# Sparse attention and gated MLP on one core: selection rows issued from ScalarE's queue, pair 0's clamp and subtraction moved, one transposed block on TensorE, a new order

## The chip, the cores and the metric

The kernel runs on 1 core of one Trainium2 chip. The metric is the device time of one execution in microseconds (us), lower is better. Its engines, as the profile names them: PE (TensorE matmuls; PEld its weight loads), DVE (VectorE), ACT (ScalarE), POOL (GpSimd) and SP (SyncE, which here only issues DMAs). An engine name with a q (SPq, ACTq) is a DMA issue on that engine's instruction stream.

## The reference, cut to what matters

```python
# attention: q, k, v are [4, 8, 768, 64]; chunks of 32 keys, nc = 24, top_k = 6
k_min, k_max = min / max of k over each chunk
ub = sum_d max(q * k_min, q * k_max)            # upper bound of a chunk for a query
ub = where(causal over chunks, ub, -1e9)
top_chunks = the 6 best chunks of each query
scores = where(chunk chosen and causal, q @ k.T / 8, -1e9)
x = softmax(scores) @ v                         # heads side by side: [4, 768, 512]
# gated MLP of x
h = gelu_tanh(x @ w_in); u, v = halves of h     # w_in [512, 1024]
v_n = (v - mean) / sqrt(var + 1e-6) * g_ln
v_s = w_sg @ v_n + b_sg                         # over the 768 positions of a batch
out = x + (u * v_s) @ w_out
```

## The kernel before, in words

The 32 heads are worked on as 16 pairs (p = 0 to 15, four pairs to a batch b). For each pair the K side (`kside`) transposes k by TensorE (`ktr`) or by a VectorE block transpose (`kbt`), takes chunk minima and maxima into the tile W (`kmm` or `kmmr`, VectorE), copies k to bf16 (`kev`, `kevh`), and subtracts the minima from the maxima (`wsub`, line 639, on POOL). The Q side (`qside`) transposes q (`qtr`), copies it from PSUM to qT (`qev`), clamps it at zero from below into rT (`rel`, line 662, on POOL, reading qT), and casts it (`qcast`). The bound is then two matmuls, qT by the minima plus rT by the differences (`ub`). VectorE transposes it (`utr`), finds the eight best of each query (`m8`), compares (`dn`) and transposes the result back into the tile Dt (`dt`, line 774).

From pair 4 on pairs go two at a time through the selection (`select_full`), and a DMA brings each head's rows of Dt into the score operand QA: `qd`, line 779, four for each couple of pairs, 24 in all, 36 KB each. The score matmuls (`sc`, line 820, three tiles of 1024, 1024 and 640 columns for each head of the pair) wait for them, ScalarE takes the exponential (`exp`, line 826), POOL zeroes above the diagonal (`aff`), TensorE multiplies by v (`pv`, `pvd`, lines 898 and 905), and VectorE divides into XS (`rcp`, line 913, and `xs`, line 915). For each pair `xtrans` transposes the 128 columns of x into xT: by six TensorE transposes and a VectorE copy (`xtr`, `xev`), or, for the blocks listed in XDMA, by one DMA transpose on SP's queue (line 924).

After every fourth pair the MLP of that batch follows: `hv` (line 947) and `gv` (gelu) for the gate half, `bns`, `bna`, `var`, `rstd` and `vhat` for the normalisation, `hu` (line 998) and `gu` for the other half, `pt` (line 1015, w_sg by vhat, which needs all six vhat of its batch), `vs` and `gt` or `gtp` for the gating, `ou` (line 1060) and `os` (line 1072) for the output, `st` for its store. Stores of batches 0 to 2 are issued on ScalarE's queue, those of batch 3 on SP's.

Nothing of this order is left to the program text. The functions only record operations, each with an engine, the tiles that it reads and writes, and a name (its tag). The five lists in TABLE give the order on each engine, as numbers of operations in the order of recording; `slots` gives the PSUM buffer of each tile (four buffers of 512 columns for most, two of 1024 for the scores). `link` puts in the semaphore waits that the order makes necessary. Every engine's list, SP's and ScalarE's DMA issues among them, is worked in order: what waits holds all that stands behind it.

Of the kernel before, what the change touches and what calls it, by code (L numbers as in the profile page):

```python
# [260 lines left out]
def _build(nc, ctx, q, k, v, w_in, g_ln, w_sg, b_sg, w_out, out):  # L261
# [55 lines left out]
    XDMA = tuple((2, d) for d in range(NDK)) + tuple((3, d) for d in range(3))  # L317
# [412 lines left out]
    def select_full(pairs, u, v_):  # L730
# [21 lines left out]
        for hf, t in enumerate(ts):  # L752
            for d0, d1 in ((0, 128),) if hf == 0 else ((0, 64), (64, 128)):
                s0 = (d0 + 64 * hf) % 128
# [3 lines left out]
                    dve(NH, 190), ("utr", pairs[0], hf), reads=[t], writes=[("U", u, hf, d0)], ps=[t])  # L758
# [23 lines left out]

    def mask_rows(w):

        for i in range(2):
# [7 lines left out]
            else:  # L793
# [3 lines left out]
                 gps(S // 2, 150), ("mrow", w, i, 2), shift=(i == 0), writes=[("QD", w, i)] + ([("QA", w, 0, 0), ("QA", w, 0, 1)] if i == 0 else []))  # L797

    def scores_full(p):
# [6 lines left out]
        for i in range(2):  # L806
            for c, c0 in enumerate(range(0, ETOT, 1024)):
# [10 lines left out]
                def sc(e, t=t, mms=mms, i=i):  # L818
                    for (o, n, kb, q0) in mms:
# [456 lines left out]
```

## Time and profile before

| | us |
|---|---|
| median of 3 runs | 214.81 |
| the runs | 214.98, 212.99, 214.81 |
| the profiled execution: its own time | 211.83 |
| the profiled execution: first to last instruction (span) | 209.7 |
| PE busy | 193.1 (92%) |
| DVE busy | 185.0 (88%) |
| ACT busy | 155.5 (74%) |
| POOL busy | 126.9 (61%) |

The profile is one execution; 2.1 us of its own time lie outside its span. Busy time of PE is the time in which at least one matmul was under way; matmuls are pipelined, so a row of the trace can be longer than what one more such instruction would add. The chain of waits follows the work that ended last back from the end, so the length of a piece in it is net of overlap. All times below count from the start of the span. The granted TensorE clock was 1.000 of full speed throughout.

### The profile page before, as it was taken

The page shows a single profiled execution, that of the slowest core. Times are in us where ns is not written, and L with a number is a line of the kernel's source. Part 1 is how long each engine was busy: PE and PEld are TensorE (multiplying, and loading weights), DVE is VectorE, ACT ScalarE, POOL GpSimd, SP SyncE. Part 2 cuts the span into 40 slices and gives each one's busy share as a digit, 9 for nine tenths or more (in the row PEclk, how much of TensorE's full clock was granted, in tenths as well). Part 3 has the DMA queues.
Part 4 walks back from the last instruction along what each step waited for, and adds up shares of the span by engine and source line. Part 5 has one row for each costly group of instructions (what it writes and reads, how often), then busy time and mean ns, then how long its engine had stood idle before and what let it go on. Part 6 is the DMA issues. An engine that isn't in the chain of part 4 may idle for free.

```text
span 209.7 us, 5781 instructions
## 1 busy us (share of the span) xinstructions
PE 193.1 (92%) x2254; PEld 125.7 (60%) x2254; DVE 185.0 (88%) x507; ACT 155.5 (74%) x221; POOL 126.9 (61%) x179
## 2 busy tenths in 40 slices
PE   7789979889999998999997999987998999899993
PEld 2446757664675775985554766763655667455652
DVE  4698999999999999999999999999798347598994
ACT  3479969974899986998898768987999974563000
POOL 7376869678378989796633597988603695111000
PEclk9999999999999999999999999999999999999999
DMA  7999999959899989979999679894006054011226
GB/s 150 219 218 237 238 289 283 322 115 201 188 197 164 216 133 185 178 138 225 205 192 167 164 153 232 138 197 104 2 7 137 0 91 137 29 74 50 100 101 252
DMA packets 106891, 33.71 MB, mean 161 GB/s; under 512 B 100976, under 2 KB 102000, under 8 KB 106864
## 3 DMA queue, kind: packets, MB, share of 16 engines
q1 hardware_dynamic: 104272, 28.62, 69.3%
q10 hardware_dynamic: 2592, 4.72, 7.0%
q8 instruction: 18, 0.29, 0.6%
q14 instruction: 9, 0.07, 0.1%
HBM read 24.77 MB, written 6.29 MB: 148 GB/s over the span
## 4 chain that ended last, share of the span: by engine, by line
PE 39%; DVE 36%; DMA 11%; ACT 5%; issue 4%; SPq 3%; DVEq 0%; POOL 0%
PE PSG L1015 8%; PE PSG L947 6%; PE PSG L1060 5%; PE PSG L998 5%; PE PSC L820 5%; DMA QA<-Dt 5%; DVE m L766 4%; DVE U L755 3%; DVE W L619 3%; DVE vgb L1036 3%; DVE XS L915 3%; DMA bsgbc<-in_moe_b_sg_dram 3%; DVE KA L791 3%; PE PSG L572 3%; PE PSG L898 2%
## 5 line engine op out<-in xcount | busy, mean ns | idle before, releaser
L826 ACT ACTIVATE E<-PSC 128x1024 bf16<-128x1024 f32 (+1 forms) x72 | 62.8, 915 | 9.7 <-PE PSC L820 8.7
L820 PE MATMUL PSC<-QA,KA 128*128 128x128 bf16 (+2 forms) x336 | 37.7, 246 | 1.8 <-DMA QA<-Dt 1.4
L1015 PE MATMUL PSG<-wsgT,vhat 128*128 128x384 bf16 x192 | 34.5, 326 | 1.4 <-DVE vhat L987 1.4
L820 PEld LDWEIGHTS PSC<-QA,KA 128*128 128x128 bf16 x336 | 23.6, 98 | 12.3 <-ACT E L826 4.5
L1040 POOL TENSOR_TENSOR uT<-vgb,uT 128x384 bf16<-128x384 f32 x24 | 22.4, 947 | 9.5 <-DVE vgb L1036 9.3
L669 POOL CAST QA<-qT 64x768 bf16<-64x768 f32 (+1 forms) x28 | 23.4, 838 | 4.0 <-DVE qT L646 2.1
L1015 PEld LDWEIGHTS PSG<-wsgT,vhat 128*128 128x128 bf16 x192 | 18.0, 98 | 12.5 <-DVE vhat L987 1.9
L998 PE MATMUL PSG<-xT,winb 128*128 128x384 bf16 x128 | 23.7, 326 | 1.2 <-DMA xT<-XS 1.2
L1003 ACT ACTIVATE uT<-PSG 128x384 bf16<-128x384 f32 x32 | 14.5, 489 | 12.9 <-PE PSG L998 12.5
L831 POOL TENSOR_SCALAR_AFFINE_SELECT E<-E 128x768 bf16<-128x768 bf16 x24 | 20.6, 863 | 5.8 <-ACT E L826 5.5
L875 ACT ACTIVATE E<-PSC 128x1024 bf16<-128x1024 f32 (+1 forms) x24 | 21.2, 917 | 3.5 <-PE PSC L866 3.5
L1060 PE MATMUL PSG<-woutb,uT 128*128 128x512 bf16 (+1 forms) x100 | 23.7, 370 | 0.0
L947 PE MATMUL PSG<-winb,xT 128*128 128x512 bf16 x96 | 22.2, 379 | 1.4 <-DVE xT L464 0.8
L965 POOL TENSOR_TENSOR rstd<-rstd,neghalf 128x3 f32<-128x3 f32 x8 | 7.3, 916 | 24.9 <-DVE rstd L963 24.8
L951 ACT ACTIVATE vgb<-PSG 128x512 f32<-128x512 f32 x24 | 13.8, 598 | 9.3 <-PE PSG L947 9.2
L898 PE MATMUL PSG<-vx,E 128*128 128x65 bf16 x480 | 19.8, 194 | 0.2
L619 DVE TENSOR_REDUCE W<-PSG 128x12 f32<-128x384 f32 x32 | 16.1, 544 | 3.8 <-POOL W L395 2.7
L898 PEld LDWEIGHTS PSG<-vx,E 128*128 128x128 bf16 x480 | 17.2, 98 | 3.0 <-DVE vgb L1036 0.5
L1036 DVE SCALAR_TENSOR_TENSOR vgb<-PSG,glnT,bsgbc 128x384 f32<-128x384 f32 x24 | 14.3, 605 | 5.3 <-PE PSG L1015 5.2
L998 PEld LDWEIGHTS PSG<-xT,winb 128*128 128x128 bf16 x128 | 12.0, 98 | 10.5 <-DMA xT<-XS 1.4
L956 DVE BATCH_NORM_STATS2 stats<-vgb 128x6 f32<-128x512 f32 x24 | 15.7, 678 | 2.2 <-ACT vgb L951 2.1
L915 DVE TENSOR_TENSOR XS<-PSG,rden 128x384 bf16<-128x384 f32 x32 | 17.2, 550 | 0.4
(94 smaller groups left out, 374.8 us busy)
## 6 DMA issues: line engine op xcount, KB each, us to landing
vn<-in_v_dram SPq DMA_DIRECT2D x16, 384.0 KB, 5.1
qn<-in_q_dram SPq DMA_DIRECT2D x24, 192.0 KB, 4.5
out_dram<-osb ACTq DMA_DIRECT2D x18, 256.0 KB, 2.5
kn<-in_k_dram SPq DMA_DIRECT2D x16, 192.0 KB, 4.5
kn<-in_k_dram SPq DMA_DIRECT2D x32, 96.0 KB, 4.0
uT<-in_moe_w_sg_dram SPq DMA_DIRECT2D x4, 384.0 KB, 5.2
vgb<-in_moe_w_in_dram SPq DMA_DIRECT2D x3, 512.0 KB, 5.6
qn<-in_q_dram SPq DMA_DIRECT2D x16, 96.0 KB, 3.9
```

What stands on the lines that cost most here:

```text
L619: P.op("dve", lambda d, m=m, op=op, src=src, h0=h0, h1=h1: d.tensor_reduce(W[w][:, m, 12 * h0:12 * h1].rearrange("p (h c) -> p h c", h=h1 ...
L669: P.op("pool", lambda g, i=i, r0=r0, r1=r1: g.tensor_copy(QA[w][i or 0][r0:r1, :], qT[r][r0:r1, :]), gps(S, 250 if i == 1 else 150), ("qca ...
L820: r = e.matmul(t.ap()[:, o:o + n], KA[w][i][:, 128 * kb:128 * kb + 128], QA[w][i][:, q0:q0 + n], start=True, stop=True)
L826: P.op("act", lambda e, t=t, c0=c0, c1=c1, i=i: e.activation(E[es][:, i, c0:c1], t.ap()[:, 0:c1 - c0], ACTF.Exp, scale=SCALE), act(c1 - c0 ...
L875: P.op("act", lambda e, t=t, c0=c0, c1=c1, n=n: e.activation(E[es][:, :, c0:c1], t.ap().rearrange("p (i x) -> p i x", i=2)[:, :, 0:n], ACT ...
L898: r = e.matmul(t.ap()[:, 65 * qb:65 * qb + 65], E[es][:, i, a:a + 128], vx[w][:, kb, i, :], start=first, stop=False, skip_group_check=True)
L915: P.op("dve", lambda d: d.tensor_tensor(XS[:, b % 2, hh // 2, :, i * DH:(i + 1) * DH], pv3()[:, :, 0:DH], rden[rs][:].rearrange("p (j o) - ...
L947: r = e.matmul(t.ap()[:, 0:F], xT[s][:, dk, 128 * qt:128 * qt + 128], winb[:, dk, F:DFF], start=(dk == 0), stop=(dk == NDK - 1))
L998: r = e.matmul(t.ap()[:, 0:TG], winb[:, dk, 128 * fb:128 * fb + 128], xT[s][:, dk, TG * tg:TG * tg + TG], start=(dk == 0), stop=(dk == NDK ...
L1015: r = e.matmul(t.ap()[:, 0:TG], vhat[s][:, sb, 128 * fb:128 * fb + 128], wsgT[:, sb, TG * tg:TG * tg + TG], start=(sb == 0), stop=(sb == N ...
L1040: P.op("pool", lambda g, xg=xg, tg=tg, fb=fb: g.tensor_tensor(gT[s][:, fb, TG * tg:TG * tg + TG], xg, uT[s][:, fb, TG * tg:TG * tg + TG], ...
L1060: r = e.matmul(t.ap()[:, 0:c1 - c0], gT[s][:, fb, 128 * qt:128 * qt + 128], woutb[:, fb, c0:c1], start=(fb == 0), stop=(fb == NF - 1))
```

## The change

- QDQ, the pairs whose `qd` rows ScalarE's queue issues, was empty and now holds pairs 4 to 15: all 24 go from SP's list to ScalarE's.
- RELA = (0,): pair 0's clamp is two Relu activations on ScalarE that read q's transposes in PSUM (`rela0,0` of 192 columns, `rela0,1` of 384), where it was one POOL instruction that read qT.
- WSD = (0,): pair 0's subtraction is on VectorE, where it was on POOL.
- XDMA loses (3, 2): block 2 of batch 3 (pair 14) is transposed by TensorE and copied by VectorE. It had seven blocks and has six.
- The bookkeeping name of a head's rows is split in two (QD with 0 and 1); with ROT = 0 both are written by the same DMA, as before. LQ, LK and ROT are new switches that are off.
- All five lists, and the PSUM buffers, are new.

```diff
-    XDMA = tuple((2, d) for d in range(NDK)) + tuple((3, d) for d in range(3))
+    XDMA = ((2, 0), (2, 1), (2, 2), (2, 3), (3, 0), (3, 1))
...
-    QDQ = ()
-    RELA = ()
-    WSD = ()
+    QDQ = (4, 5, 6, 7, 8, 9, 10, 11, 12, 13, 14, 15)
+    LQ = ()
+    LK = ()
+    RELA = (0,)
+    ROT = 0
+    WSD = (0,)
...
                 P.op("act" if p in QDQ else "sp", lambda e, w=w, i=i, g0=g0: e.dma_start(
                     QA[w][i][g0:g0 + 32, LO:S], Dt[v_][g0:g0 + 32].rearrange("p a b -> p (a b)")), dmac(590),
-                    ("qd", p, i), reads=[("Dt", v_)], writes=[("QD", w, i)], dma=f"qd{w}_{i}", xfer=150)
+                    ("qd", p, i), reads=[("Dt", v_)], writes=[("QD", w, i, 0), ("QD", w, i, 1)], dma=f"qd{w}_{i}", xfer=150)
...
```

The lists themselves, read back into tags. A name is followed by pair or batch, then head and piece. First ScalarE up to pair 0's exponentials; the init names are constant set-up (init10 and 11 copy the tile IND, which POOL finishes with `init8` and `init9`; init21 copies 32 columns):

```
before  init22 init21 init12 qev0,0 qev0,1 kev0,0 kev1,1 init11 kev1,0 qev1,1 qev1,0 init10 kev0,1 exp0,0
after   init22 init10 qev0,0 init21 rela0,0 rela0,1 qev0,1 kev0,0 init12 init11 kev0,1 kev1,1 kev1,0 qev1,0 qev1,1 exp0,0
```

On PE both lists begin ktr0,0 ktr0,1 qtr0,0 qtr0,1 ktr1,1 ktr1,0 ub0, and ub0 has the PSUM buffer that ktr0,0 had. ktr1,0 now has the buffer of qtr0,1. On POOL two memsets of 64x384 that stood behind `init9` now stand ahead of it. VectorE's list has kmm1,1,1 kmm1,0,0 kmm1,0,1 kmm1,1,0 utr0,0.

Where the `qd` rows stand on ScalarE's list, by the number of exponentials ahead of the first row of each couple of pairs:

```
pairs           4,5   6,7   8,9   10,11   12,13   14,15
exps ahead       24    33    45      57      69      83
```

VectorE around `dt14`, `rcp12` and batch 2's normalisation:

```
before  ... bns2,0 rcp12,1 bns2,1 xs12,1 utr14,0 utr14,1 bna2,1 ufix14 rcp12,0 utr14,1 xs12,0 m814,0 m814,1 kevh15,1 dn14 bna2,0 dt14 ...
after   ... bns2,0 bns2,1 bna2,0 bns2,2 utr14,0 utr14,1 utr14,1 ufix14 m814,1 m814,0 dn14 bna2,1 dt14 bna2,2 var2,0 bns2,4 bns2,3 kevh15,1 bna2,3 vhat2,2 rcp12,1 vhat2,0 vhat2,1 xs12,1 ...
```

PE from the first `pt2` to the first `hv3`:

```
before  pt2,0,0 pt2,1,0 sc14,1,0 sc14,0,0 pv13,0 pvd13,0 pt2,1,2 pt2,1,1 sc15,0,0 pt2,0,1 sc14,1,2 pt2,0,2 sc14,0,1 sc14,0,2 pt2,0,3
        sc15,0,1 pv14,1 pvd14,1 pv14,0 pvd14,0 sc15,1,2 sc15,0,2 pt2,1,3 pv15,1 pvd15,1 pv15,0 pvd15,0 ou2,1 ou2,0 xtr3,3 ou2,2 hv3,0
after   pt2,0,3 pt2,0,0 pt2,1,0 pt2,0,1 sc15,1,2 sc14,0,0 pt2,1,3 sc15,1,0 pvd14,1 pt2,1,1 sc14,0,2 pt2,0,2 sc15,0,1 sc15,0,0 pv14,0
        pvd14,0 pv15,1 pvd15,1 sc15,0,2 pt2,1,2 pv15,0 pvd15,0 xtr3,2 ou2,1 xtr3,3 ou2,2 hv3,0
```

## Rows read from the trace of the kernel before

**Rows 1.** Busy time by stretch: us, PE, PEld, DVE, ACT, POOL, clock, DMA, GB/s

```profile
13.00:50.00 37.00, 32.70 (x605) 23.38 (x606) 35.03 (x113) 29.65 (x42) 29.30 (x39) 1.00 1.04 243
50.00:100.00 50.00, 48.84 (x572) 34.03 (x571) 49.40 (x129) 44.09 (x67) 39.28 (x54) 1.00 0.98 181
100.00:143.00 43.00, 40.80 (x483) 26.48 (x482) 42.32 (x115) 36.44 (x48) 29.22 (x38) 1.00 0.97 183
143.00:163.00 20.00, 18.03 (x194) 10.98 (x193) 17.46 (x56) 18.68 (x26) 8.53 (x12) 1.00 0.20 45
163.00:177.00 14.00, 13.83 (x192) 10.23 (x190) 7.42 (x17) 11.08 (x14) 10.18 (x12) 1.00 0.30 72
```

**Rows 2.** Timeline (start, us, engine, line), vhat of batch 2 and first pt2

```profile
160.10 1.91 DVE L987 TENSOR_SCALAR vhat<-vgb,mv,rstd 128x512 bf16<-128x512 f32 x4
...
162.06 2.12 PE L1015 MATMUL PSG<-wsgT,vhat 128*128 128x384 bf16 x12
```

**Rows 3.** DMA queue's own waits on SP: us in total, times, longest

```profile
SPq L779 <- DVE Dt L774: 14.5, 2, 14.2
```

**Rows 4.** The lines 779 and 1078: duration ns min/median/max; issue to landing of line 779

```profile
L779 SPq DMA_DIRECT2D QA<-Dt x24: 507/590/1666, 53.6 to 158.7; - x24
...
DMA to landing us min/median/max: 1.8/2.5/3.9
...
L1078 ACTq DMA_DIRECT2D out_dram<-osb x18: 338/338/452, 93.5 to 201.3; - x18
```

**Rows 5.** Timeline, a store issued by ScalarE between two exponentials

```profile
174.38 0.70 ACT L826 ACTIVATE E<-PSC 128x640 bf16<-128x640 f32 x1 [0.43 <-PE PSC L820]
...
174.66 0.34 ACTq L1078 DMA_DIRECT2D out_dram<-osb  x1
...
174.99 0.70 ACT L826 ACTIVATE E<-PSC 128x640 bf16<-128x640 f32 x1
```

**Rows 6.** Timeline, ScalarE and VectorE where Dt of pairs 6 and 7 is ready

```profile
72.44 1.59 ACT L826 ACTIVATE E<-PSC 128x640 bf16<-128x640 f32 x2
...
73.26 0.78 DVE L774 STREAM_TRANSPOSE Dt<-Dn 128x576 bf16<-128x576 bf16 x1
```

**Rows 7.** Timeline of the start

```profile
3.95 0.21 ACT L440 ACTIVATE CMw<-CMw 64x32 bf16<-64x32 bf16 x1
...
4.55 0.41 POOL L796 MEMSET QA<- 64x384 uint32 x1
...
5.77 0.84 ACT L425 ACTIVATE IND<-IND 32x768 bf16<-32x768 bf16 x1 [1.61 <-POOL IND L421]
...
7.11 0.87 ACT L461 ACTIVATE qT<-PSG 128x384 f32<-128x384 f32 x2 [0.50 <-PE PSG L572]
...
7.87 0.50 ACT L461 ACTIVATE KA<-PSG 128x384 bf16<-128x384 f32 x1
...
9.18 0.69 PE L699 MATMUL PSG<-qT,W 64*32 64x288 f32 x8
...
10.80 0.47 DVE L709 STREAM_TRANSPOSE U<-PSG 128x288 f32<-128x288 f32 x1
```

**Rows 8.** Waits of VectorE from 8 to 163 us: total, times, longest

```profile
DVE rden L913 <- PE PSG L905: 0.9, 1, 0.9
```

**Rows 9.** Pieces of the chain that ended last: start, us, what

```profile
31.27 0.46 PE PSG L932 x6
...
147.86 0.46 PE PSG L898 x15
...
180.38 5.34 PE PSG L947 x24
```

**Rows 10.** Timeline before hv3; then line 924's issue to landing

```profile
175.51 1.25 SPq L924 DMA_TRANSPOSE xT<-XS  x1
...
180.38 5.34 PE L947 MATMUL PSG<-winb,xT 128*128 128x512 bf16 x24 [0.57 <-DVE osb L1072]
...
DMA to landing us min/median/max: 3.1/4.4/5.1
```

More of the change, by code (lines that the diff above doesn't have):

```diff
@@ L541, in load_slices @@
                 g = 2 * i + dh
-                o = P.op("sp", lambda e, i=i, dh=dh, g=g: e.dma_start(
+                o = P.op("act" if p in (LK if nm == "kn" else LQ) else "sp", lambda e, i=i, dh=dh, g=g: e.dma_start(
                     flat[32 * g:32 * g + 32], bass.AP(src.tensor, (2 * p + i) * S * DH + 32 * dh,
@@ L752, in select_full @@
         for hf, t in enumerate(ts):
-            for d0, d1 in ((0, 128),) if hf == 0 else ((0, 64), (64, 128)):
-                s0 = (d0 + 64 * hf) % 128
+            for d0, d1 in ((0, 128),) if hf == 0 or ROT else ((0, 64), (64, 128)):
+                s0 = (d0 + 64 * hf) % 128 if not ROT else d0
                 P.op("dve", lambda d, hf=hf, t=t, d0=d0, d1=d1, s0=s0: d.transpose(
@@ L757, in select_full @@
                     t.ap()[s0:s0 + d1 - d0, 0:NH]),
-                    dve(NH, 190), ("utr", pairs[0], hf), reads=[t], writes=[("U", u, hf, d0)], ps=[t])
+                    dve(NH, 190), ("utr", pairs[0], hf), reads=[t], writes=[("U", u, hf, d0)] + ([("U", u, hf, 64)] if ROT else []), ps=[t])
             if hf == 0:
@@ L778, in select_full @@
                 w, g0 = p % NW, 32 * (2 * (1 - i) + x)
+                if ROT:
+                    for hf in range(2):
+                        g1 = (g0 + 64 * hf) % 128
+                        P.op("act" if p in QDQ else "sp", lambda e, w=w, i=i, g0=g0, g1=g1, hf=hf: e.dma_start(
+                            QA[w][i][g0:g0 + 32, LO + NH * hf:LO + NH * hf + NH], Dt[v_][g1:g1 + 32, hf, :]), dmac(590),
+                            ("qd", p, i, hf), reads=[("Dt", v_)], writes=[("QD", w, i, hf)], dma=f"qd{w}_{i}{hf}", xfer=150)
+                    continue
                 P.op("act" if p in QDQ else "sp", lambda e, w=w, i=i, g0=g0: e.dma_start(
                     QA[w][i][g0:g0 + 32, LO:S], Dt[v_][g0:g0 + 32].rearrange("p a b -> p (a b)")), dmac(590),
-                    ("qd", p, i), reads=[("Dt", v_)], writes=[("QD", w, i)], dma=f"qd{w}_{i}", xfer=150)
+                    ("qd", p, i), reads=[("Dt", v_)], writes=[("QD", w, i, 0), ("QD", w, i, 1)], dma=f"qd{w}_{i}", xfer=150)
     def mask_rows(w):
@@ L796, in mask_rows @@
             P.op("pool", lambda g_, i=i, m0=m0: g_.memset(QA[w][i][m0:m0 + 64, :].bitcast(mybir.dt.uint32), 0),
-                 gps(S // 2, 150), ("mrow", w, i, 2), shift=(i == 0), writes=[("QD", w, i)] + ([("QA", w, 0, 0), ("QA", w, 0, 1)] if i == 0 else []))
+                 gps(S // 2, 150), ("mrow", w, i, 2), shift=(i == 0), writes=[("QD", w, i, 0), ("QD", w, i, 1)] + ([("QA", w, 0, 0), ("QA", w, 0, 1)] if i == 0 else []))
     def scores_full(p):
@@ L823, in scores_full @@
                 P.op("pe", sc, pe(*[m_[1] for m_ in mms]), ("sc", p, i, c),
-                     reads=[("KA", w, i, 0), ("KA", w, i, 1), ("QA", w, i, 0), ("QA", w, i, 1), ("QD", w, i), ("KI", w, i)],
+                     reads=[("KA", w, i, 0), ("KA", w, i, 1), ("QA", w, i, 0), ("QA", w, i, 1), ("QD", w, i, 0), ("QD", w, i, 1), ("KI", w, i)],
                      writes=[t], alloc=t)
@@ L1149 @@
     "pe": (
[15 rows of a table removed]
-    "act": (
[10 rows of a table removed]
-    "dve": (
[16 rows of a table removed]
-    "pool": (
[15 rows of a table removed]
[15 rows of a table added]
+    "act": (
[11 rows of a table added]
+    "dve": (
[16 rows of a table added]
+    "pool": (
[14 rows of a table added]
     "slots": (
-        "0123032020231012132120211200011020133021011010202001210101011330013101100033031200120322232211111021"
-        "1302331211110010002211010013021301010121322011100032303200123110233001312002233203011011100100011103"
-        "2101010013231100101201321320011322030301021123010201100123010100010101002310011113330120302103233302"
-        "110231233021"),
+        "0123032020133213212013202110101103022120110001001300131010012330300111000233321102212021101302322102"
+        "2120211230011010032130010100221010011031322111000300132031212212303333021231112201000101301101101020"
+        "1310101003001001011323230320011320113200002021301310011123010001200100113130111012013102302210201013"
+        "3002302121321"),
     "filler": (
```

110 rows, old and new, of the table TABLE are left out of this document.

## The prediction, made before the changed kernel was run

> **What bounds the kernel now.** I read the busy time by stretch first [rows 1], because the shares over the whole span (PE 92%, DVE 88%) hide that the bound changes. From 13 to 143 us VectorE is busy 35.03 + 49.40 + 42.32 = 126.75 of 130 us, so it idles 3.25 us in all; nothing can shorten that part by more unless VectorE gets less work. From 143 to 163 three engines are close together: VectorE 17.46, PE 18.03 and ScalarE 18.68 of 20. From 163 to 177 PE is busy 13.83 of 14 and VectorE only 7.42, and from there to the end PE works almost without a gap. The turning point shows in the timeline [rows 2]: the last four vhat of batch 2 end at 160.10 + 1.91 = 162.01 and the first pt2 starts at 162.06. So the time is VectorE's work up to the last vhat2, and then PE's work behind it. An edit counts only if it takes from VectorE's list ahead of vhat2, from VectorE's waits there, or from PE's list behind it.
>
> The SP queue's own waits come next [rows 3]: SP stood 14.5 us for Dt, and that is what the moved rows free. It looks like a prize, but VectorE, which uses the loads, hardly waited in those stretches [rows 1].
>
> **The change part by part.** The sum is made against the profiled execution's 211.83 us. The median of the runs shown is 2.98 us above it, and the same sum is then put on the median.
>
> *The 24 qd rows.* SP loses 24 issues of 0.590 us (median), 14.2 us of its time, and the Dt waits; worth nothing, as the loads are no bound. ScalarE gains 24 issues. Its own stores take 0.338 us each to issue [rows 4], and they cost nothing where they stand between two exponentials: the store at 174.66 lies inside the exponential that runs from 174.38 to 175.08, and the next begins at 174.99 [rows 5]. I take nothing for the issue. Cover is the activation in front; without it the price is 24 x 0.59 = 14.2 us of ScalarE's time. The wait for Dt is the other half, since behind a waiting row stand exponentials, the K copies and the gelus, and PE's score buffers wait for them. In the trace before, pairs 6 and 7's Dt was ready at 73.26 + 0.78 = 74.04, when 24 + 11 = 35 exponentials were through (the two from 72.44 end at 74.03) [rows 6]; the new list puts its first row behind 33. Counted in the same way along the timeline, of whose five such places this one stands in the rows, for pairs 8, 10, 12 and 14 the trace had 44, 57, 69 and 83 through; the new list has 45, 57, 69 and 83. So a row is reached about when its Dt is there, and only at pairs 6 and 7 would ScalarE stand for some two exponentials. Between 50 and 100 it has 50 - 44.09 = 5.91 us idle for that. I take nothing; the upper end is the second rival's.
>
> The rows land in 1.8 to 3.9 us from SP's queue [rows 4]. The Trainium skill ("DMA: Bandwidth & Descriptors", section "Issuing engines are not separate DMA queues") says that DMAs of all issuing engines share the same 16 DMA engines, and that issuing from several saves only the sequencers' issue time. By it the transfers land no sooner and the part is worth nothing, as I have it; no row here shows the same transfer from both queues.
>
> *Pair 0's clamp and subtraction.* On ScalarE, ahead of kev0,0, stand now qev0,0, init21, the two clamps and qev0,1. From the first at 7.11: 0.44 + 0.21 + about 0.3 (192 columns, between 0.21 and 0.44) + 0.44 + 0.44, and kev0,0's 0.50, is 9.44 us [rows 7]. If init10, which ended at 6.61, comes two memsets of 0.41 later it ends at 7.43 and adds 0.32: 9.76. ub0 has the PSUM buffer that kev0,0 reads, so it starts at 9.44 to 9.76 where it started at 9.18, and utr0 follows it. I take +0.5 us; the ends are 0 (VectorE finds other work) and +0.6. The subtraction (24 columns) is new on VectorE: between nothing and 0.47, a transpose of 288 columns [rows 7]; I take +0.2.
>
> *Block (3, 2).* Six transposes more on PE, at a net 0.46 us for six [rows 9], in the part where PE sets the end: +0.46. The copy on VectorE is hidden by ou2,1 and ou2,2 (four of the 24 matmuls that take 5.34 make 0.89 us [rows 9], and one copy is about half of it); uncovered it costs some 0.5. The DMA that goes was issued at 175.51 and landed by 178.6 to 180.6 (3.1 to 5.1 after) [rows 10]; hv3 began at 180.38 after 0.57 idle, but the row names another releaser. I take nothing for it, and keep -0.57 as the end.
>
> *The new order, middle (13 to 143).* VectorE's list has the same operations in nearly the same order: summed by their durations, each dt comes within 1.2 us of where it stood, and exactly the subtraction is added ahead of the last vhat2. I take nothing; the ends are plus and minus the 3.25 us of idle time there.
>
> *The new order, 143 to 163.* Before, VectorE stood 0.9 us for PE at rcp12 [rows 8], with pairs 14 and 15's selection queued behind. Now rcp12 comes behind dt14 and the first vhat2, and two more score tiles (82 for 80) stand ahead of the first hv2 or hu2. I take -0.9; the ends are 0 and all of VectorE's idle time there, 20 - 17.46 = 2.54.
>
> *The new order behind the first pt2.* Compare PE's lists from there to hv3. Before: nine score tiles (five of 1024 columns, four of 640) and the v products of five heads. Now: seven (four and three) and three heads with one pvd more. Net prices [rows 9]: 5.34 / 24 = 0.2225 us for 512 columns, so 0.445 and 0.278 a tile; 0.46 for a pv (15 matmuls), 6/15 of it, 0.18, for a pvd. Tiles: 0.445 + 0.278 = 0.72. Heads: 5 x 0.64 - (3 x 0.64 + 0.18) = 1.10. Together -1.82 us. That work moves ahead of vhat2, where PE idles 20 - 18.03 = 1.97 us [rows 1], so it just fits. Ends: 0, if it does not fit, and -1.82.
>
> *Sum:* 0.5 + 0.2 + 0.46 - 0.9 - 1.82 = -1.56 us: 211.83 becomes 210.3, and the median 214.81 becomes **213.2 us**.
>
> **The rivals.**
>
> *The waits go too (faster).* The order takes the rest of VectorE's idle time from 143 to 163 (2.54 - 0.9 = 1.64) and the 0.57 ahead of hv3: 213.25 - 2.21 = 211.0 us. For it: the waits are few and at places where the list changed. Against: every wait that goes leaves room for the next, with three engines over 87% there.
>
> *ScalarE becomes the bound (slower).* From 50 to 143 it has 93 - 44.09 - 36.44 = 12.47 us idle, and 20 rows fall in that time. If a row holds ScalarE 12.47 / 20 = 0.62 us, issue and wait for Dt together, ScalarE is full and starts to set the time; from 0.81 on, the kernel is over 1% slower (20 x 0.81 - 12.47 = 3.7, on 213.25). At 0.85, an uncovered 0.59 and a wait of 0.26, it is 17 - 12.47 = 4.5 us: 217.8 us. For it: SP's rows took up to 1.666 us to issue [rows 4], and the two exponentials at pairs 6 and 7. Against: rows 5, and the counts.
>
> *Nothing moves (no change).* The two score tiles can come earlier only if their exponentials do. Those are 1024 and 640 columns; one of 640 takes 0.70 [rows 5], so the two about 1.7 us, and ScalarE has 20 - 18.68 = 1.32 idle from 143 to 163. If that holds them, -1.82 falls away: 213.25 + 1.82 = 215.1 us. The Trainium skill's rule above points the same way, as it leaves the moved rows without an effect.
>
> **How the numbers follow.** Forecast 0.38, waits go 0.28, ScalarE bound 0.18, nothing moves 0.16. About 1%, 2.15 us, is what a measurement of this kernel can tell from no change. Faster by over that (under 212.7): the 0.28, and 0.10 of the forecast's own spread (211.6 to 214.2, from its ends at 143 to 163): 0.38. Slower: the 0.18 and 0.02 of the last rival: 0.20. Within 1%: 0.42. The range goes from 209.4 (the faster rival and half of the middle's 3.25) to 217.0 (where ScalarE holds a row 0.8 us); outside lies some 0.15, most of it the ScalarE case.
>
> **What would show each step.** ScalarE's row issues: inside the activation before, with no idle time in front of the next; a wait of ScalarE for Dt of over 2 us would speak for the slower rival, as would ScalarE busy or held through all of 50 to 143. The first ub0 at 9.4 to 9.8 and utr0 half a us later than before. VectorE still over 97% busy from 13 to 143. No wait of VectorE at rcp12. From the end of the last vhat2 to the first hv3 matmul: 180.38 - 162.01 = 18.4 us before, 17.0 if the tail's sum holds (-1.82 + 0.46). What would make it wrong: the last vhat2 later than 162.0 by over 2 us, or a hole in PE's work between it and hv3.

## The result, and the profile after

| | before | changed |
|---|---|---|
| median, us (20 runs each) | 213.30 | 216.59 |
| lowest to highest | 210.53 to 215.75 | 213.65 to 218.87 |
| the profiled execution, its span | 211.83, 209.7 | 217.69, 215.8 |
| PE busy, DVE busy, ACT busy | 193.1, 185.0, 155.5 | 193.8, 186.4, 155.9 |

The changed kernel is slower, by a ratio of 1.0146 (95% interval 1.0107 to 1.0185). The forecast had it 1.6 us faster than the median that it was set against (213.2 for 214.81); over 20 runs the medians differ by 3.3 us the other way. The two traces lie 5.9 us apart and the medians 3.3, since the profiled execution of before was 1.5 us under its median and that of after 1.1 over it: the traces tell where the time goes, the medians how much. A ratio here leaves out runs over 1.5% above the fastest of their kernel, so it can differ a little from the quotient of the medians.

Busy time by stretch of the changed kernel, columns as in [rows 1]:

```profile
13.00:50.00 37.00, 33.02 (x610) 23.90 (x611) 34.11 (x115) 30.37 (x45) 28.31 (x39) 1.00 1.10 256
50.00:100.00 50.00, 44.05 (x538) 30.75 (x538) 46.50 (x123) 38.58 (x58) 37.27 (x48) 1.00 1.00 184
100.00:143.00 43.00, 39.65 (x424) 24.93 (x427) 40.09 (x109) 34.27 (x46) 28.88 (x36) 1.00 0.75 144
143.00:163.00 20.00, 19.15 (x213) 11.59 (x213) 18.48 (x52) 18.37 (x25) 13.01 (x18) 1.00 0.35 83
163.00:177.00 14.00, 12.97 (x159) 9.38 (x157) 9.21 (x24) 13.50 (x18) 5.83 (x7) 1.00 0.34 69
```

The work is nearly the same, the gaps are not. From 50 to 143 us VectorE now idles 93 - 46.50 - 40.09 = 6.4 us (1.3 in [rows 1]) and PE 93 - 44.05 - 39.65 = 9.3 (3.4). ScalarE is not full there either: it idles 20.2 us (12.5 before).

What VectorE (8 to 163 us) and PE (13 to 163) waited for; us in total, times, longest:

```profile
DVE rden L923 <- PE PSG L915: 4.7, 6, 1.9
```

```profile
PE PSC L830 <- DMA QA<-Dt: 4.1, 4, 1.6
PE PSC L830 <- ACT E L836: 2.2, 4, 0.9
```

VectorE's wait of [rows 8], 0.9 once, has become 4.7 in six: `rcp` (now line 923) waits for PE's `pvd`, PE's scores (line 830) wait for rows and for exponentials. The rows of Dt, as in [rows 4]:

```profile
L789 ACTq DMA_DIRECT2D QA<-Dt x24: 514/528/613, 54.2 to 170.4; - x24
...
DMA to landing us min/median/max: 1.8/4.3/7.3
```

Issuing one takes 0.528 us, less than on SP (0.590). But it lands 4.3 us after its issue in the median, where SP's took 2.5. The place of [rows 6], pairs 6 and 7, in the timeline (start, us; what it waited for in brackets):

```profile
70.62 1.62 ACT L836 ACTIVATE E<-PSC 128x640 bf16<-128x640 f32 x2
...
72.66 0.77 DVE L777 STREAM_TRANSPOSE Dt<-Dn 128x576 bf16<-128x576 bf16 x1
...
73.46 0.51 ACTq L789 DMA_DIRECT2D QA<-Dt  x1
74.02 0.84 ACT L594 ACTIVATE KA<-IND 64x768 bf16<-64x768 f32 x1 [1.78 <-DVE vgb L1046]
74.04 1.22 ACTq L789 DMA_DIRECT2D QA<-Dt  x2
75.31 0.70 ACT L836 ACTIVATE E<-PSC 128x640 bf16<-128x640 f32 x1 [0.44 <-issue]
```

ScalarE stands from 72.24 to 74.02 for the first row: until 73.43 because Dt is not there, then for the issue (the brackets name other releasers; that the row holds ScalarE is read from the start of its issue, 0.03 us after Dt's end). The next activation covers one row and a part of the second, and ScalarE stands 0.44 us more. Such holds came before 74.02, 91.96, 123.20 and 140.24 (1.78, 1.23, 1.70 and 1.76 us).

The tail, to be held against [rows 2] and [rows 10]: last vhat2, first pt2, hv3.

```profile
168.21 1.45 DVE L997 TENSOR_SCALAR vhat<-vgb,mv,rstd 128x512 bf16<-128x512 f32 x3
...
170.67 1.63 PE L1025 MATMUL PSG<-wsgT,vhat 128*128 128x384 bf16 x9
...
185.56 2.11 PE L957 MATMUL PSG<-winb,xT 128*128 128x512 bf16 x9
```

The last vhat2 ends at 169.66, 7.65 us later than before; from there to hv3 it is 15.9 us, where it was 18.4. Not all of that is gained: hv3 to the end of the span takes 30.2 us, where it took 29.3. From the last vhat2 to the end it is 46.1 for 47.7, so the loss lies ahead of vhat2 and the tail is 1.6 us shorter.

### The profile page after: what moved, and what is told of

It is laid out like the page before. It is cut to its first block, busy times and chain, and to the rows that moved or that the text cites. A ratio compares the mean times of both kernels' runs of the same rounds, so it can differ in the third digit from the quotient of the medians.

```text
span 215.8 us, 5765 instructions
## 1 busy us (share of the span) xinstructions
PE 193.8 (90%) x2248; PEld 126.3 (59%) x2260; DVE 186.4 (86%) x509; ACT 155.9 (72%) x223; POOL 128.5 (60%) x177
## 4 chain that ended last, share of the span: by engine, by line
DVE 33%; PE 33%; ACT 15%; DMA 10%; issue 4%; SPq 3%; ACTq 1%; DVEq 0%
ACT E L836 7%; PE PSG L1070 6%; PE PSG L1025 6%; DMA QA<-Dt 5%; PE PSG L957 5%; ACT E L885 5%; PE PSC L830 4%; DVE m L769 4%; DVE U L758 3%; PE PSG L1008 3%; DMA kn<-in_k_dram 3%; DVE vhat L997 3%; PE PSG L908 2%; SPq L559 2%; DVE stats L966 2%
## 5 line engine op out<-in xcount | busy, mean ns | idle before, releaser
L841 POOL TENSOR_SCALAR_AFFINE_SELECT E<-E 128x768 bf16<-128x768 bf16 x24 | 21.5, 901 | 13.4 <-ACT E L836 12.8
L1025 PEld LDWEIGHTS PSG<-wsgT,vhat 128*128 128x128 bf16 x192 | 18.0, 98 | 11.2 <-DVE vgb L1046 0.5
L1070 PE MATMUL PSG<-woutb,uT 128*128 128x512 bf16 (+1 forms) x90 | 21.7, 370 | 1.0 <-DVE XS L925 0.4
L1013 ACT ACTIVATE uT<-PSG 128x384 bf16<-128x384 f32 x32 | 15.0, 491 | 10.0 <-PE PSG L1008 8.4
L677 POOL CAST vx<-vn 128x768 bf16<-128x768 f32 x16 | 14.7, 929 | 3.5 <-DMA vn<-in_v_dram 3.4
```

Of the source, the lines that this page charges most:

```text
L841: P.op("pool", lambda g, ev=ev: g.affine_select(ev, ev, pattern=[[0, NT], [1, 128]], compare_op=ALU.is_ge, fill=0.0, base=0, channel_multi ...
L1025: r = e.matmul(t.ap()[:, 0:TG], vhat[s][:, sb, 128 * fb:128 * fb + 128], wsgT[:, sb, TG * tg:TG * tg + TG], start=(sb == 0), stop=(sb == N ...
L1070: r = e.matmul(t.ap()[:, 0:c1 - c0], gT[s][:, fb, 128 * qt:128 * qt + 128], woutb[:, fb, c0:c1], start=(fb == 0), stop=(fb == NF - 1))
```

## The experiments

Every run was timed beside the kernel before on the same chip. Each was run 6 to 12 times. "Mean difference" is the mean of all its runs less that of before's, with twice its standard error, in us.

| run | median | before | ratio (95% interval) | mean difference |
|---|---|---|---|---|
| rows_only | 213.79 | 213.42 | 1.0067 (1.0026 to 1.0109) | +0.55 ± 0.74 |
| rows_only_held | 214.83 | 213.42 | 1.0080 (1.0036 to 1.0125) | +1.32 ± 1.00 |
| new_rows_on_sp | 217.50 | 213.42 | 1.0211 (1.0146 to 1.0276) | +4.62 ± 1.93 |
| after_held | 216.96 | 213.42 | 1.0164 (1.0092 to 1.0237) | +3.59 ± 1.84 |
| new_first_56 | 213.96 | 213.87 | 1.0028 (0.9958 to 1.0098) | -0.03 ± 1.29 |
| old_first_56 | 216.59 | 213.87 | 1.0237 (1.0168 to 1.0305) | +2.86 ± 0.96 |
| old_first_144 | 218.12 | 213.87 | 1.0278 (1.0158 to 1.0398) | +4.02 ± 1.47 |
| new_first_144 | 218.69 | 213.87 | 1.0338 (1.0217 to 1.0459) | +5.45 ± 1.65 |
| before_no_rows | 210.31 | 213.26 | 0.9916 (0.9880 to 0.9952) | -2.67 ± 0.72 |
| after_no_rows | 211.13 | 213.26 | 0.9934 (0.9887 to 0.9981) | -2.28 ± 0.90 |
| new_rows_on_sp2 | 217.73 | 213.26 | 1.0265 (1.0214 to 1.0317) | +4.77 ± 0.85 |
| old_first_104 | 216.67 | 213.26 | 1.0152 (1.0102 to 1.0202) | +3.82 ± 1.30 |
| after_rows_aside | 212.97 | 213.00 | 1.0011 (0.9972 to 1.0051) | -0.15 ± 0.64 |
| before_rows_aside | 211.97 | 213.00 | 0.9964 (0.9923 to 1.0005) | -1.09 ± 0.78 |
| after_rows_ready | 211.92 | 213.00 | 0.9945 (0.9906 to 0.9985) | -0.56 ± 0.86 |
| new_rows_on_sp3 | 214.31 | 213.00 | 1.0052 (1.0014 to 1.0091) | +1.39 ± 0.83 |
| new_rows_on_sp4 | 211.39 | 213.31 | 0.9927 (0.9878 to 0.9977) | -2.09 ± 0.92 |

The changed kernel itself stands at +3.04 ± 0.83 in this measure. Differences between two rows of this table are uncertain by some 1 to 1.3 us where each kernel ran 11 times or more. The two measures differ by up to 2.2 us in a row, so where a reading rests on the size, both are given; a ratio of 1.01 is 2.1 us.

### Rows or order: four first runs

**rows_only**: before, with its rows on ScalarE (MOVE puts an operation behind another one on its engine's list; all 24 rows stand in it).

```diff
-    QDQ = ()
+    QDQ = (4, 5, 6, 7, 8, 9, 10, 11, 12, 13, 14, 15)
+MOVE = {("qd", 4, 0): ("qev", 7, 0), ("qd", 5, 1): ("gv", 0, 5),
...
```

> The order of before, with one part of the change: pairs 4 to 15 have their 24 rows issued by ScalarE, each row behind the activation that was running when its Dt was written in the trace of before. SP keeps its list without the rows, so nothing on SP waits for Dt any more. Three theories of the 1.46% that the changed kernel is slower by (3.1 us of 213.3). Theory L (landing): SP's loads, no longer held behind the wait for Dt, stand in front of the rows on the same DMA engines, the rows land 1.5 to 2 us later (4.3 instead of 2.5 us in the median), and scores wait: here +2 to +4 us, with a median landing above 3.5 us. Theory S (ScalarE): the landing matters little; ScalarE stands still at the rows, for Dt and for issue, in the middle of the exps: here +2 to +4 us as well. Theory O (order): the rows are free as forecast and the new order of the rest costs the time: here within 0.5 us of before.

The rows alone, each placed where its Dt is ready, cost 0.55 ± 0.74 us; by the ratio it is 1.4 us (0.6 to 2.3). That is less than theories L and S said, by the ratio more than theory O did, and the landing was 3.4 us. One place shows the harm; PE, ScalarE and VectorE in its timeline:

```profile
94.74 0.61 PE L820 MATMUL PSC<-QA,KA 128*128 128x384 bf16 x4 [1.24 <-DMA QA<-Dt]
95.39 2.11 ACT L826 ACTIVATE E<-PSC 128x1024 bf16<-128x1024 f32 x2 [1.44 <-PE PSC L820]
96.03 0.27 DVE L913 RECIPROCAL rden<-PSG 128x6 f32<-128x6 f32 x2 [1.98 <-PE PSG L905]
```

A row that lands 1.24 us late becomes 1.44 us of ScalarE and 1.98 of VectorE.

**rows_only_held**: the same, and 16 loads of SP wait for Dt.

```diff
+        for load, dt in HOLD.items():
+            P.ops[tag[load]].deps.add(tag[("dt", dt)])
```

> The kernel of the run rows_only, and besides, the loads that stood behind the rows on SP's list in before wait for the same Dt on which the rows waited there (16 loads), so that SP is held about as long as before (14.5 us) and its loads come no earlier. ScalarE issues the rows as in rows_only. Theory L: rows land as in before (median near 2.5 us), the loss of rows_only is gone, within 1 us of before. Theory S: as slow as rows_only, +2 to +4 us, since ScalarE stands at the same places. Theory O: within 0.5 us of before, as rows_only.

What SP waited for (us in total, times, longest):

```profile
SPq L564 <- DVE Dt L774: 13.3, 1, 13.3
SPq L542 <- DVE Dt L774: 6.3, 2, 4.4
```

SP was held for Dt even longer than in [rows 3] (19.6 us), yet the landing stayed at 3.4 us and nothing was won. That SP's loads leave earlier and so push the rows back, theory L's mechanism, is not borne out. That loads which leave beside the rows, once Dt is there, delay them is not excluded.

**new_rows_on_sp**: the new order with `QDQ = ()`, rows behind kn8,1,1, vn7,0, kn12,1,1, qn15,1,0, kn14,1,1 and vn15,0 on SP's list.

> The changed kernel with its order on every engine, its first pair, its x^T block on TensorE, but the 24 rows of pairs 4 to 15 back on SP's list, four at a time behind the load that SP had come to when ScalarE issued them in the trace of the changed kernel. SP is held for Dt again, ScalarE is not. Theories L and S: the loss goes, and what is left is the tail's gain: between 1 us slower and 2 us faster than before (ratio 0.990 to 1.005). Theory O: still 2 to 4 us slower than before (ratio 1.010 to 1.019).

Slower still, against theories L and S, but not a fair trial: SP came to the rows of pairs 6 and 7 only 3.7 us after Dt, and PE stood for one:

```profile
82.74 1.01 PE L830 MATMUL PSC<-QA,KA 128*128 128x128 bf16 x7 [4.63 <-DMA QA<-Dt]
```

**after_held**: the changed kernel with the two lines of HOLD above, for wb0, kn10,0,1, vn8,0, kn14,0,1, xtr2,1 and xtr3,1.

> The changed kernel with one wait more at six places of SP's list: the load that SP issued next when the rows of a couple of pairs were due (pairs 4/5, 6/7, 8/9, 10/11, 12/13, 14/15) now waits for the Dt of that couple. ScalarE issues the rows as in the changed kernel. Theory L: SP's loads no longer overtake the rows, which land in about 2.5 us in the median instead of 4.3, and 2 us or more of the 3.1 come back (ratio to before 0.995 to 1.006). Theory S: nothing comes back, ScalarE stands as before at its rows (ratio 1.010 to 1.019). Theory O: nothing comes back either, or it is slower still, since loads come later (1.010 to 1.025).

No gain. It decides little: the profile gives SP 0.5 us of waits for Dt in all, since SP reached most of these loads when Dt was there.

### Where in the kernel: joints of the two orders

Each kernel takes the operations that one kernel starts first, in its order, and the rest in the other's; the PSUM buffers of the second part are renamed so that the order can run. For new_first_56:

```diff
-    XDMA = ((2, 0), (2, 1), (2, 2), (2, 3), (3, 0), (3, 1))
+    XDMA = tuple((2, d) for d in range(NDK)) + tuple((3, d) for d in range(3))
-    QDQ = (4, 5, 6, 7, 8, 9, 10, 11, 12, 13, 14, 15)
+    QDQ = (4, 5)
...
```

> A joint of the two orders: the 416 operations that the changed kernel begins with (to the middle of the first u projection, about 57 us; first pair, start and the rows of pairs 4 and 5 on ScalarE as changed) in its order, all the others in the order of before, with their rows on SP and x^T as before. Theory M: the time is lost by the new order of the middle; then this is within 1 us of before. Theory B: it is lost at the beginning already (a start that is only seemingly as early); then +2 to +4 us. Theory G: the tail's shorter stretch is a true gain of about 2 us, lost here since the tail is that of before; no more than 1 us from before here as well.

> The joint the other way round at the same place: the 412 operations that before begins with (to about 57 us; pair 0 as before, the rows of pairs 4 and 5 on SP) in its order, all the others in the new order, the rows of pairs 6 to 15 on ScalarE, the x^T block on TensorE. Theory M: slower than before by what the changed kernel is, +2 to +4 us. Theory B: within 1 us of before. Theory G: as theory M.

> The joint late: the 1,027 operations that before begins with (to the middle of the v projection of x tile 2, about 150 us) in its order with the rows of pairs 4 to 13 on SP; what is left, the last pairs, tile 2's end, the whole of tile 3, in the new order, rows of pairs 14 and 15 on ScalarE, x^T block on TensorE. Theory M: the loss is gone, within 1 us of before. Theory G: the tail is truly shorter, 1.8 (as forecast) to 3.4 us (as the trace of the changed kernel has it) faster than before, and faster than both kernels. Theory B: as theory G or M, since no beginning is changed.

> The late joint the other way round: the first 985 operations of the changed kernel in its order (to about 150 us, rows of pairs 4 to 13 on ScalarE), what is left in the order of before (rows of pairs 14 and 15 on SP, x^T of tile 3 by DMA). Theory M without a gain in the tail: as the changed kernel, +2 to +4 us over before. Theory G: the changed kernel's loss without its gain, +5 to +6.5 us. Theory B: as theory M.

The new beginning shows no cost (-0.03 ± 1.29); with the old one and the rest new it is +2.86 ± 0.96, the whole loss (5.0 us by the ratio, more than the whole). So pair 0's edits and the rows of pairs 4 and 5 don't make it. Both late joints lost 4 to 5.5 us. For new_first_144 that is what theory G said; old_first_144 went against all three, with PE idle 5.0 us from 143 to 163, at the joint itself. So they say nothing sure of the tail. A joint at 109 us (QDQ = pairs 10 to 15):

> A joint of the two orders in the u projection of x tile 1, at about 109 us of before: the first 769 operations in the order of before with the rows of pairs 4 to 9 on SP, the rest in the new order with the rows of pairs 10 to 15 on ScalarE and the x^T block on TensorE. In the traces TensorE stood 4.3 us longer between 73 and 100 us in the changed kernel than in before and 2.6 us longer between 122 and 143, and less long elsewhere. If the stretch from 57 to 109 us makes the loss (both theories allow it): within 1 us of before. If the later stretch makes it: +2 to +4 us. The joint itself may cost something, as both joints at 150 us seem to have done.

The later half alone makes the loss as well, and the first exponentials of its three couples come 4.3, 6.0 and 5.0 us after Dt, as late as in the changed kernel or later (the next table says how that is taken). So it is not one place but something that the later couples share; that it is the rows, the next runs test.

### Without rows

```diff
+        skip = {o.idx for o in P.ops if o.tag[0] == "qd" and o.tag[1] >= 4}
+        for o in P.ops:
+            o.deps -= skip
...
+            order[e] = [i for i in order[e] if i not in skip]
```

> The kernel before with the 24 rows of pairs 4 to 15 left out: they are not copied, nothing waits for them, SP is not held for Dt, and the scores of these pairs work on the rows of pairs 0 to 3 that lie in the buffers (so the selection of pairs 4 to 15 is left out; the work of all other instructions is the same). What the rows cost in the old order: SP's hold is behind loads that are early, so 0 to 1.5 us faster than before. It is the yardstick for the run after_no_rows.

> The changed kernel with the same 24 rows left out in the same way: ScalarE issues no rows and waits for no Dt, and no score waits for a row. Theory W (rows): the changed kernel is slower because of its rows, through ScalarE's standing and late landings together; then it comes to within 1 us of before_no_rows, and 2.5 to 5 us under the changed kernel. Theory O (order): it stays 2 to 3.5 us slower than before_no_rows, and is no more than 1.5 us faster than the changed kernel.

Theory W holds: without rows the two kernels are level (-2.67 and -2.28). The rows cost 2.7 ± 0.7 us in before, more than the 0 to 1.5 expected, and 3.04 + 2.28 = 5.3 ± 1.2 us in the changed kernel. By the ratios it is 1.8 and 4.5 us.

### Standing or landing

**after_rows_aside** and **before_rows_aside** send the rows where nobody reads them:

```diff
-                    QA[w][i][g0:g0 + 32, LO:S], Dt[v_][g0:g0 + 32]...
+                    QS[g0:g0 + 32, :] if p >= 4 else QA[w][i][g0:g0 + 32, LO:S], Dt[v_][g0:g0 + 32]...
```

> The changed kernel; ScalarE issues the 24 rows of pairs 4 to 15 at the same places and waits for the same Dt, but they land in a tile of their own that nothing reads, and no score waits for them (the selection of pairs 4 to 15 is left out, as in after_no_rows). Only ScalarE's standing (wait for Dt and 0.53 us of issue a row) and the traffic are left of the rows. Without rows this kernel was 2.3 us faster than before, with them 3.0 slower, so 5.3 us are to be shared out. Theory S (ScalarE's standing makes them): +1.5 to +3 us over before, as the changed kernel. Theory L (late landing makes them): 1 to 2.5 us faster than before, as after_no_rows.

> The same with the kernel before: SP issues the 24 rows at their places and is held for Dt as ever, they land in the tile of their own, no score waits for them. Without rows the kernel was 2.7 us faster than before. If SP's hold (14.5 us in all) makes these 2.7 us: within 0.7 us of before. If the landings make them: 2 to 3 us faster than before, as before_no_rows.

**after_rows_ready** takes the wait for Dt away: ahead of the rows' loop,

```diff
+        v_ = (v_ - 1) % 4
```

> The changed kernel with each row copied from the Dt of the couple of pairs before its own, which has been ready for 15 us or more (so the selection of pairs 4 to 15 is another than the reference's). ScalarE issues the rows at the same places, never waits for Dt, and the scores wait for the landings. In the trace of the changed kernel ScalarE stood some 4 us for Dt. If that hold is the cause: within 1 us of before, or faster. If the time of issue (0.53 us a row in front of the exps) or the landing is: +1.5 to +3 us over before.

Of the 5.3 us, ScalarE's standing alone makes 2.28 - 0.15 = 2.1; that the scores also wait for the landing adds 3.2 (1.6 and 2.9 of 4.5 by the ratios). Neither theory has it all. In before, on SP, it is again between the two: of 2.67 us SP's hold makes 1.6 and the landing 1.09 (1.0 and 0.8 by the ratios). Each share is uncertain by about 1 us, so that a held ScalarE costs more than a held SP isn't shown; the landing's share comes out larger in the changed kernel. With rows that never wait for Dt, which leave up to 2.3 us ahead of it, 3.6 of the 5.3 are gone (4.3 of 4.5), though ScalarE still issues all 24 and they still land in 4.3 us. The cost is a chain in series: Dt, ScalarE's turn, issue, landing, score, exponential. To see it, I set the 72 exponentials of pairs 4 to 15 in the trace beside their order in ScalarE's list, and took the time from the end of Dt's transpose to the first exponential of the first and of the second head that follows (us):

| kernel | pairs 6, 7 | 8, 9 | 10, 11 | 12, 13 | 14, 15 |
|---|---|---|---|---|---|
| after_no_rows | 5.3, 7.4 | 3.8, 5.3 | 3.0, 4.0 | 3.4, 4.2 | 3.8, 10.2 |
| after_rows_ready | 5.3, 7.4 | 3.8, 5.8 | 3.0, 5.1 | 3.7, 4.4 | 4.8, 11.2 |
| after_rows_aside | 6.1, 8.1 | 4.4, 6.4 | 4.0, 5.2 | 4.7, 5.4 | 5.0, 11.4 |
| changed kernel | 7.6, 9.7 | 5.4, 8.1 | 4.4, 6.7 | 4.8, 5.4 | 5.0, 11.4 |
| new_rows_on_sp4 | 5.3, 7.4 | 4.0, 6.1 | 4.2, 5.1 | 3.4, 4.2 | 3.2, 9.6 |
| before | 4.2, 5.1 | 3.5, 17.1 | 3.4, 6.1 | 3.2, 4.9 | 3.7, 4.6 |

Without rows the new order has its first exponentials 3.0 to 5.3 us after Dt. In the changed kernel every couple comes 1.2 to 2.3 us later, the second heads 1.2 to 2.8. At pairs 12 to 15 standing alone (after_rows_aside) makes all of it; that the scores wait for the landing shows at pairs 6 to 11. Couple 12, 13 in the trace, without rows, then changed (Dt; what ScalarE does next):

```profile
135.12 0.78 DVE L777 STREAM_TRANSPOSE Dt<-Dn 128x576 bf16<-128x576 bf16 x1
...
136.20 1.02 ACT L836 ACTIVATE E<-PSC 128x1024 bf16<-128x1024 f32 x1 [0.28 <-PE PSC L830]
```

```profile
137.59 0.78 DVE L777 STREAM_TRANSPOSE Dt<-Dn 128x576 bf16<-128x576 bf16 x1
...
138.40 1.80 ACTq L789 DMA_DIRECT2D QA<-Dt  x3
140.24 1.02 ACT L836 ACTIVATE E<-PSC 128x1024 bf16<-128x1024 f32 x1 [1.76 <-DVE XS L925]
```

Three rows in a row, 1.80 us, and the exponential that had followed the last one after 0.28 us of idle time now follows after 1.76 (the bracket names XS, which was written by then; the exponential starts 0.04 us after the third issue).

### The new order with prompt rows on SP

**new_rows_on_sp2**, **3** and **4** repeat new_rows_on_sp with other places on SP's list (the operation that a couple's first row stands behind; two to a line here):

```diff
-    ("qd", 6, 0): ("vn", 7, 0),    ("qd", 8, 1): ("kn", 12, 1, 1),
+    ("qd", 6, 0): ("wo", 2),       ("qd", 8, 1): ("qn", 11, 0, 0),
-    ("qd", 10, 0): ("qn", 15, 1, 0),    ("qd", 12, 1): ("kn", 14, 1, 1),
+    ("qd", 10, 0): ("vn", 11, 0),       ("qd", 12, 1): ("vn", 12, 0),
```

These are the places of 4. In 2, pairs 8 and 9 stood behind kn12,0,0 and the last two as in the first trial; in 3, 8 and 9 stood behind kn11,0,0, 10 and 11 as in 4, and 12 and 13 behind kn14,1,1. (Counted on the list, 2 moved pairs 6 and 7 up by four loads and 3 moved pairs 8 and 9 by eight, not by three and ten as the expectations say.)

> The run new_rows_on_sp again, with the rows of pairs 6 and 7 three loads earlier on SP's list and those of pairs 8 and 9 two loads: in that run SP came to the rows of pairs 6 and 7 only 3.7 us after their Dt, and TensorE stood 4.63 us for one of them, so it was no fair trial. Theory W: without that wait, and with ScalarE free of rows, it comes to within 1 us of before or is up to 2 us faster. Theory O: still 2 to 3.5 us slower than before.

Slower than both theories said (+4.77), and again no fair trial: SP came to the rows of pairs 8 and 9 5.3 us after Dt, and PE stood 5.59 us (the bracket names no row; that it was one follows from the place). For pairs 10 and 11 it stood 2.80.

```profile
96.76 0.69 PE L830 MATMUL PSC<-QA,KA 128*128 128x256 bf16 x3 [5.59 <-issue]
```

After that stand the granted clock was 0.50 from 96 to 102 us, which is part of the loss (columns as in [rows 1], the third from the right is the clock):

```profile
96.00:102.00 6.00, 5.24 (x63) 5.02 (x64) 1.30 (x5) 1.85 (x3) 0.00 (x0) 0.50 0.80 161
```

> The changed kernel with its rows on SP, as new_rows_on_sp2, the rows of pairs 8 and 9 now ten loads earlier than there, and those of pairs 10 and 11 three, since SP came to them 5.3 and 0.8 us after Dt there, and TensorE stood 5.6 and 2.8 us. At the rows of pairs 12 to 15, which SP issued 0 to 1.9 us after Dt, the first exps came as soon as with no rows at all. Theory W (what counts is that all rows leave within 2 us of Dt, and not on ScalarE): between 2 us faster than before and 1 us slower. Theory O: +2 us or more.

From pair 6 on all rows left within 2.7 us of Dt: +1.39 in place of +4.77, between what the two theories said. PE's longest wait was now that of a q transpose whose load had been held behind the rows:

```profile
95.06 0.52 PE L575 MATMUL PSG<-identF,qn 128*128 128x128 f32 x3 [2.11 <-DVE XS L925]
```

> The changed kernel with its rows on SP as in new_rows_on_sp3, the rows of pairs 8 and 9 two loads later than there (SP stood idle from 86.5 to 88.55 us there in front of them, and the q load behind them came late: TensorE stood 2.11 us at 95 us), those of pairs 12 and 13 one load earlier. new_rows_on_sp3 was 1.4 us (0.6 to 2.2) slower than before. If that stand was its main remainder: within 1 us of before. If the new order has a cost of its own that no place of the rows mends: again 1 to 2 us slower.

It is faster than both kernels: 0.9927 (0.9878 to 0.9977) of before. It is the best of four sets of places, each mended by the trace of the one before. Against the same order without rows (-2.28) its rows cost 0.2 ± 1.3 us. That the load was the releaser in 3 is inferred from SP's timeline (the row names XS); the move took the stand away. Busy time by stretch, then the rows, then vhat2, pt2 and hv3:

```profile
13.00:50.00 37.00, 34.25 (x616) 24.18 (x615) 34.30 (x116) 31.06 (x47) 28.75 (x39) 1.00 1.08 255
50.00:100.00 50.00, 47.16 (x561) 32.93 (x560) 49.49 (x128) 42.17 (x62) 40.27 (x53) 1.00 0.97 179
100.00:143.00 43.00, 42.08 (x496) 27.97 (x495) 40.67 (x113) 37.52 (x50) 29.26 (x39) 1.00 1.00 184
143.00:163.00 20.00, 19.21 (x228) 11.85 (x227) 18.26 (x58) 19.70 (x27) 9.63 (x13) 1.00 0.16 46
```

```profile
L789 SPq DMA_DIRECT2D QA<-Dt x24: 513/592/1364, 53.7 to 155.4; - x24
...
DMA to landing us min/median/max: 1.8/2.5/3.7
```

```profile
160.04 1.45 DVE L997 TENSOR_SCALAR vhat<-vgb,mv,rstd 128x512 bf16<-128x512 f32 x3
...
161.72 4.07 PE L1025 MATMUL PSG<-wsgT,vhat 128*128 128x384 bf16 x24
...
176.62 5.34 PE L957 MATMUL PSG<-winb,xT 128*128 128x512 bf16 x24
```

PE's idle time from 50 to 143 is 3.8 us (9.3 changed, 3.4 before), vhat2 ends at 161.49 (162.01 before), and the tail to hv3 is 15.1 us. From the last vhat2 to the end of the span it is 45.3 us (47.7 before).

## Why the prediction was wrong, point by point

**The 24 rows: the step that failed.** "I take nothing for the issue" and "I take nothing" for the wait for Dt. The difference between the changed kernel and new_rows_on_sp4, which differ only in the rows' queue and places, is 3.04 + 2.09 = 5.1 ± 1.2 us (4.7 by the ratios). Three things went wrong in it. First, counting exponentials told roughly when ScalarE reaches a row, but Dt came 1.1 us behind at pairs 10 and 11 and 1.2 at 6 and 7, and it takes no more. (The count at pairs 6 and 7 is off by one: 34 exponentials were through, not 35.) Second, the cover of [rows 5] is one activation in front: 0.70 to 1.02 us hide one row, and rows stand two and three in a row. Third, the landing was taken over from SP; it was 4.3 us, not 2.5. The Trainium skill ("DMA: Bandwidth & Descriptors", section "Issuing engines are not separate DMA queues") says that another issuing engine saves only issue time. The trace agrees that the transfers land no sooner: 4.3 us for 2.5.

Behind all three stands "worth nothing, as the loads are no bound". The chain that ended last, from which [rows 9] took its prices, ran through the rows three times already before the change, 9.5 us in all (start, us, what):

```profile
88.95 2.73 DMA QA<-Dt
...
133.76 3.65 DMA QA<-Dt
...
156.25 3.10 DMA QA<-Dt
```

The 5.1 us are the price of queue and places together. In before's order the same move cost 0.55 ± 0.74 (rows_only; 1.4 by the ratio). No run gave the rows other places on ScalarE's list in the new order, so what the queue alone costs there is open.

**ScalarE as the bound.** The slower rival had the right engine and came near in size (217.8, which is 3.0 over the median that it was set against; 3.3 over before's was measured), but by another mechanism. It priced ScalarE's capacity, to be used up at 0.62 us a row. ScalarE never ran out: it idled 20.2 us from 50 to 143. What broke was the time from Dt to the first exponentials. So it decided at a lower price than I had put on it, and that the size came out is luck. (By the rival's own sum the end of the range, 0.8 us a row, is 216.8 and not 217.0.)

**SP's freed time.** "It looks like a prize" but is none: right. rows_only frees SP of it and is no faster. In new_rows_on_sp4 the rows are back on SP, which again stands 18.5 us at their line (22.0 before, the 14.5 of [rows 3] among them; 12.4 of the 18.5 are put down to `rstd`, ahead of the rows of pairs 14 and 15), and yet it is faster than before.

**Pair 0, +0.7 in all.** kev0,0 ended at 9.21 and utr0 began at 10.87 (10.80 in [rows 7]): the two clamps took 0.71 together and init10 was not late, so +0.07 for the +0.5. The subtraction took 0.18 us ahead of a wait of VectorE of 0.48, so it shows no cost. new_first_56 has the whole beginning at -0.03 ± 1.29, which agrees with both.

**Block (3, 2) and the tail.** Forecast 17.0 us from vhat2 to hv3; measured 15.9 in the changed kernel and 15.1 in new_rows_on_sp4. That isn't more gain than forecast: the comparison of PE's lists overlooked `ou2,0`, which stands ahead of hv3 before the change and behind it after. It is four of the 512-column matmuls, 0.89 us by the prediction's own price, and hv3 to the end takes 0.9 us more (30.2 for 29.3). To the end of the span the tail gained 1.6 us in the changed kernel, 2.4 in new_rows_on_sp4, and 1.3 in after_no_rows against before_no_rows; forecast 1.36. So this part was right in sign and about in size; the +0.46 can't be told apart in it, and no run tried the block alone.

**143 to 163.** The waits at `rcp` did not go: from 8 to 163 us they came to 4.7 us in six. In 143 to 163 itself it is 1.1 in two (0.9 in [rows 8]), but the changed kernel is some 5 us behind there, and other work stands in the stretch. They went where the rows were prompt: in new_rows_on_sp4 VectorE waits for no `pvd` from 50 to 163.

**The sum.** -1.56 us without the rows' price. new_rows_on_sp4, which does not pay it, measured -2.09 ± 0.92. But its rows also leave SP sooner than before's do (within 2.7 us of Dt from pair 6 on, where before's last row of pairs 8 and 9 left 12 us after), and no run gave before's rows new places. With no rows in either order the new one gains nothing (-2.28 against -2.67, 0.4 ± 1.2 slower), though its tail is 1.3 us shorter in the traces. So that the other terms were right in sum is not shown: the tail's was, and "I take nothing" for the new order from 13 to 143 may hide a loss. The one term that is clear of the noise is the rows', taken as nothing and measured at 5 us, and the chance of 0.20 for slower was too small.

## What to carry to other kernels

A small DMA between two steps of a dependent chain is priced by the time from its input to the first reader of its output, not by the busy time of the queue that issues it: ask for each how soon its reader follows, and what else stands on that engine's list then. The chain that ended last, read before the change, tells whether the transfer is on it. Put it on the queue that can stand still, just where its input comes, with the loads that are needed next in front of it: on SP such rows cost 0.2 ± 1.3 us here (2.7 ± 0.7 at before's places, in its order), and a few places on that list were worth 3 to 7 us. An engine with idle time is no free place for a DMA if its own next instruction is on the same chain.

## What the runs showed of the hardware

The same 36 KB row landed in 2.1 to 3.0 us in the median in the six traces in which SP issued all of them, and in 3.4 to 4.3 in the six in which ScalarE did, even when SP was held beside them (rows_only_held). The difference lies in the rows of pairs 4 to 11, which leave while SP's loads run: 5.2 us in the changed kernel for 2.5 before, up to 130 us. The eight rows after that land in 1.9 us in the changed kernel and in 3.1 before. Why is open.

In rows_only_held PE did nothing from 159.4 to 162.2 us, for a row, and its granted clock fell. Columns as in [rows 1], the clock is the third from the right:

```profile
158.00:160.00 2.00, 0.67 (x9) 0.39 (x7) 1.97 (x9) 1.84 (x4) 1.08 (x1) 1.00 1.88 190
160.00:162.00 2.00, 0.00 (x0) 0.00 (x0) 1.78 (x4) 1.36 (x2) 0.00 (x0) 0.69 0.10 12
162.00:164.00 2.00, 1.80 (x8) 0.96 (x9) 0.00 (x0) 0.73 (x1) 0.00 (x0) 0.50 0.00 0
...
168.00:170.00 2.00, 2.00 (x20) 1.41 (x19) 0.62 (x1) 1.97 (x3) 1.36 (x2) 1.00 0.00 0
```

At 0.50 it ran at the lower of its two levels, 1.2 GHz, until some time between 166 and 168 us: a late row can cost a second time. The granted clock was 0.50 too after PE's stands in new_rows_on_sp (4.63 us; 83 to 85.5), new_rows_on_sp2 (5.59; 96 to 102) and new_rows_on_sp3 (2.11; 96 to 99).
